# A fused transformer kernel on one Trainium2 core: the second and third group's layernorms in fixed order, their tiles in two product buffers, the third x group loaded ahead of Wk, and the first head sum two V chunks later

## The chip, the cores and the metric

The kernel runs on one core of one Trainium2 chip. The metric is the time on the device in microseconds (us) of one execution. Executions of one kernel mostly agree within 0.3%. The changes told of here are smaller than 1%, so that medians of several fast runs are compared, and the traces are read to a tenth of a microsecond.

## The reference

Two layers are applied twice to x of 2048 rows by 1024 columns (bf16). Layer A is a layernorm, a sliding-window attention with dilation and 32 heads, and a residual. Layer B is a layernorm, a feed-forward of width 3584 with GELU, and a residual.

```python
def _A_ref(x, wqkv, wo):                       # H = 32, Dh = 32, W = 8, dil = 2
    q, k, v = split_heads(x @ wqkv)            # (cut)
    idx = pos[:, None] - (jnp.arange(W) * dil)[None, :]   # 8 keys: s, s-2, ..., s-14
    logits = jnp.einsum("bhsd,bhswd->bhsw", q, kg) * scale
    attn = softmax(where(idx >= 0, logits, -1e9))
    o = jnp.einsum("bhsw,bhswd->bhsd", attn, vg)
    return merge_heads(o) @ wo
def _B_ref(x, w1, b1, w2, b2):
    return gelu(x @ w1 + b1) @ w2 + b2
x = x + _A_ref(_layernorm(x), A_wqkv, A_wo)
x = x + _B_ref(_layernorm(x), B_w1, B_b1, B_w2, B_b2)   # and both once more
```

## The kernel before

The 2048 rows are worked on in four groups of 512 (four tiles of 128 rows each); two layers make eight units, n = 0 to 7. What matters here is the first unit, some 70 us at the start, where everything has to be fetched and prepared at once.

TensorE (PE) makes Q, K and V of a group in 8 chunks each, by `gen_qkv`. One `yield` stands after each chunk, and `stage` runs "side" work after a numbered chunk. Chunks 0 to 7 are Q, 8 to 15 K, 16 to 23 V.

```python
def gen_qkv(n, parts=1, defer=False, qk_pool=None, v_late=False):
    ...
    wq = wq_first if n == 0 else load_qkv(0)
    wk = load_qkv(1)              # two loads of 1 MB
    if n == 0:
        ln_a(1)                   # layernorm of the second group
        load_x(2)                 # x of the third group
        wv = load_qkv(2)
    ...                           # 8 Q chunks
    for c in range(NCH):
        ps = qkv_chunk(wk, c, xnT)
        act.copy(kT[:, c, HALO:], ps[:])
        if not defer:
            new_prod(n, c)
        yield
    ...                           # 8 V chunks
```

The logits are not matmuls of Q and K. VectorE (DVE) multiplies Q with eight shifted views of K, chunk by chunk, into a product of 4096 columns, and adds the products pairwise in a tree. `head_sum` then has PE sum over the elements of a head with a matrix of zeros and ones. With `parts=2`, chunks 0 to 3 make a first sum and chunks 4 to 7 a second. Each product lives in one of the three buffers of the pool `bigp`.

```python
def new_prod(n, c):
    prod = bigp.tile([P, W, T], BF16, name="big")          # bufs=3
    vec.tensor_tensor(out=prod[:], in0=q_chunk_broadcast, in1=k_windows, op=ALU.mult)
    ...                            # adds to the tree after every second chunk
```

A layernorm is statistics on VectorE, rstd on GpSimd (POOL), the normalisation `xn` on VectorE, and a transposing DMA from `xn` to `xnT`, the form that PE reads. Here `xn` has three buffers of its own, and the tile framework's scheduler orders the instructions on VectorE:

```python
def ln_norm(t, mv, rstd):
    xn = lnp.tile([P, D], BF16, name="xn", bufs=3)
    vec.tensor_scalar(out=xn[:], in0=x[t][:], scalar1=mv[:, 0:1], scalar2=rstd[:],
                      op0=ALU.subtract, op1=ALU.mult)
    return xn
...
    sp.dma_start_transpose(xnT[:, tt, :, :], xn[:].rearrange("s (k p) -> s k p", p=P))
```

All loads and transposing DMAs (not the biases) are issued in order by one queue, SP's. The stages at the start:

```python
load_bias()                        # b1 and b2, on GpSimd's queue
with tc.tile_pool(name="early", bufs=1) as early:
    load_x(1)
    stage(gen_qkv(0, 2), sides=at(6, ln_a, 2, early) + at(7, load_x, 3)
          + at(14, transpose_bias) + at(19, head_sum, 0, False))   # first sum after V chunk 3
    q1 = gen_qkv(1, 2, defer=True, qk_pool=early)
    stage(q1, sides=at(5, attend, 0) + ...)                        # second sum in attend
```

Of the kernel before, what the change touches and what calls it, by code (L numbers as in the profile page):

```python
# [11 lines left out]
BF16 = mybir.dt.bfloat16  # L12
# [5 lines left out]
def kernel(  # L18
# [18 lines left out]
    P = 128  # L37
    _, S, D = A_x.shape
# [10 lines left out]
    NTT = T // P  # L49
# [20 lines left out]
    lnp = ctx.enter_context(tc.tile_pool(name="lnp", bufs=2))  # L70
    xnp = ctx.enter_context(tc.tile_pool(name="xnp", bufs=2))
    attp = ctx.enter_context(tc.tile_pool(name="attp", bufs=1))
    bigp = ctx.enter_context(tc.tile_pool(name="bigp", bufs=3))
# [30 lines left out]
    vec, act, pool, sp = InOrder(nc.vector), InOrder(nc.scalar), InOrder(nc.gpsimd), InOrder(nc.sync)  # L104
# [17 lines left out]
    def load_x(g, t0=0, t1=NTT):  # L122
        for tt in range(t0, t1):
            t = g * NTT + tt
            sp.dma_start(x[t][:], x_in[t * P:(t + 1) * P, :])

    def load_qkv(which):
        tiles = []
        for h in range(2):
            wt = wpool.tile([P, KD // 2, D], BF16, name="wt")  # L130
            sp.dma_start(wt[:], wqkv_v[:, h * (KD // 2):(h + 1) * (KD // 2), which * D:(which + 1) * D])
            tiles.append(wt)
        return tiles
# [41 lines left out]

    b1_rows = attp.tile([KF, P], BF16, name="abc")

    def load_bias():
        pool.dma_start(b1_rows[:], B_b1.rearrange("(j p) -> j p", p=P))
        pool.dma_start(b2bc[:], B_b2.unsqueeze(0).to_broadcast([P, D]))  # L180

    def transpose_bias():
# [5 lines left out]
    def ln_stats(t, mv=None, rstd=None, between=None):  # L188
        stats = lnp.tile([P, 2, 6], F32, name="stats")
        for h in range(2):  # L190
            vec.bn_stats(stats[:, h, :], x[t][:, h * HALF:(h + 1) * HALF])
            if h == 0 and between is not None:
                between()
        if mv is None:
            mv = lnp.tile([P, 2], F32, name="mv")
            rstd = lnp.tile([P, 1], F32, name="rstd")
        vec.bn_aggr(mv[:], stats[:])
        pool.tensor_tensor(out=rstd[:], in0=mv[:, 1:2], in1=eps_t[:], op=ALU.add)
        pool.tensor_tensor(out=rstd[:], in0=rstd[:], in1=mhalf[:], op=ALU.pow)
        return mv, rstd  # L200
# [2 lines left out]
        for tt in range(NTT):  # L203
            ln_stats(g * NTT + tt, mv_ahead[:, tt, :], rstd_ahead[:, tt, :])

    def ln_norm(t, mv, rstd):
        xn = lnp.tile([P, D], BF16, name="xn", bufs=3)
        vec.tensor_scalar(out=xn[:], in0=x[t][:], scalar1=mv[:, 0:1], scalar2=rstd[:], op0=ALU.subtract, op1=ALU.mult)
        return xn

    def transpose_on_pe(xn, out, pst=None, halves=1):
        if pst is None:
            pst = psum.tile([P, KD, P], BF16, name="acc", bufs=6)
        for k in range(KD):
            pe(nc.tensor.transpose(pst[:, k, :], xn[:, k * P:(k + 1) * P], ident[:]))  # L215
        n = KD // halves
        for h in range(halves):
            act.copy(out[:, h * n:(h + 1) * n, :], pst[:, h * n:(h + 1) * n, :])
# [7 lines left out]
    def ln_tile(t, tt, xnT, on_pe=False, ahead=False):  # L226
        mv, rstd = (mv_ahead[:, tt, :], rstd_ahead[:, tt, :]) if ahead else ln_stats(t)
        xn = ln_norm(t, mv, rstd)
        if on_pe:
            late.append((xn, xnT[:, tt, :, :]))  # L230
            return
        sp.dma_start_transpose(xnT[:, tt, :, :], xn[:].rearrange("s (k p) -> s k p", p=P))
# [28 lines left out]
    def new_xnT(pool=None):  # L261
        return (pool or xnp).tile([P, NTT, KD, P], BF16, name="xnT")
# [7 lines left out]
    xa = {}  # L270
    xb = {}

    def qkv_chunk(wts, c, xnT, ps=None, k0=0, k1=KD, t0=0, t1=NTT):
        if ps is None:
            ps = acc_tile()
        for k in range(k0, k1):
            mm(ps[:, t0 * P:t1 * P], lhsT=wts[k // (KD // 2)][:, k % (KD // 2), c::NCH], rhs=xnT[:, t0:t1, k, :],
               start=(k == 0 and t0 == 0), stop=(k == KD - 1), skip_group_check=t1 - t0 < NTT)
        return ps
# [21 lines left out]
    def new_prod(n, c):  # L301

        s = st[n]
        prod = bigp.tile([P, W, T], BF16, name="big")
        vec.tensor_tensor(out=prod[:], in0=s["qT"][:, c, :].unsqueeze(1).to_broadcast([P, W, T]), in1=win(s["kT"][:, c, :]), op=ALU.mult)
        tree = s["prods"]
        tree.append(prod)
        if c % 2 == 1:
            for _ in range(1 if c % (NCH // s["parts"]) == 1 else 2):
                b = tree.pop()  # L310
                vec.tensor_tensor(out=tree[-1][:], in0=tree[-1][:], in1=b[:], op=ALU.add)

    def gen_qkv(n, parts=1, defer=False, qk_pool=None, v_late=False):
        g = n % NG
        xnT = xa.pop(n)
        s = st[n]
        s["parts"] = parts
        s["prods"] = []
        qk_pool = qk_pool or attp
        wq = wq_first if n == 0 else load_qkv(0)  # L320
        wk = load_qkv(1)
        if n == 0:
            ln_a(1)
            load_x(2)
            wv = load_qkv(2)
        qT = qk_pool.tile([P, NCH, T], BF16, name="qT")
        first = {}
        for kq in range(4 if n == 0 else 0):
            for c in range(6):
                first[c] = qkv_chunk(wq, c, xnT, first.get(c), kq * (KD // 4), (kq + 1) * (KD // 4), 0, 2)  # L330
                if (kq, c) in ((1, 5), (2, 5)):
                    transpose_on_pe(*first_late.pop(0))
        for c in range(NCH):
            ps = qkv_chunk(wq, c, xnT, first[c], t0=2) if c in first else qkv_chunk(wq, c, xnT)
            act.copy(qT[:, c, :], ps[:])
            yield
        if n > 0 and not v_late:
            wv = load_qkv(2)
        kT = qk_pool.tile([P, NCH, HALO + T], BF16, name="kT")
        s["qT"], s["kT"] = qT, kT  # L340
        act.copy(kT[:, :, 0:HALO], (zhalo if g == 0 else khalo)[:])
# [6 lines that stand above are left out]
        if g + 1 < NG:  # L348
            act.copy(khalo[:], kT[:, :, T:T + HALO])
        vT = attp.tile([P, NCH, HALO + T], BF16, name="vT", bufs=2)  # L350
        s["vT"] = vT
        if v_late:
            wv = load_qkv(2)
        act.copy(vT[:, :, 0:HALO], (zhalo if g == 0 else vhalo)[:])
        for c in range(NCH):
            ps = qkv_chunk(wv, c, xnT)
            act.copy(vT[:, c, HALO:], ps[:])
            yield
        if g + 1 < NG:
            act.copy(vhalo[:], vT[:, :, T:T + HALO])  # L360
# [121 lines left out]
    def ln_a(n, pool=None, ahead=False):  # L482
        xa[n] = new_xnT(pool)
        for tt in range(NTT):
            ln_tile((n % NG) * NTT + tt, tt, xa[n], ahead=ahead)

    def stage(gen, count=None, sides=()):


        u = 0  # L490
        while count is None or u < count:
            if next(gen, gen) is gen:
                break
            for v, f in sides:
                if v == u:
                    f()
            u += 1
        for v, f in sides:
            if v >= u:
                f()  # L500

    def at(u, f, *args, **kwargs):
        return [(u, lambda: f(*args, **kwargs))]

    def each(f, n, u0, du, c0=0, c1=NCH):
        return [(int(u0 + du * (c - c0)), lambda c=c: f(n, c)) for c in range(c0, c1)]
# [4 lines left out]
    warm_up(16)  # L511
    ln_first()
    build_constants()
    load_bias()
    with tc.tile_pool(name="early", bufs=1) as early:
        load_x(1)
        stage(gen_qkv(0, 2), sides=at(6, ln_a, 2, early) + at(7, load_x, 3)
              + at(14, transpose_bias) + at(19, head_sum, 0, False))
        q1 = gen_qkv(1, 2, defer=True, qk_pool=early)
        stage(q1, sides=at(5, attend, 0) + at(5, spread, 0) + at(5, hold) + each(new_prod, 1, 8, 1, 0, 4) + each(av, 0, 12, 1))  # L520
        q2 = gen_qkv(2, defer=True)
        stage(q2, 18)
        stage(gen_wo(0, 2))
        stage(q2, sides=each(new_prod, 1, 0, 1, 4, 8) + at(3, head_sum, 1, False) + at(4, transpose_late))
# [11 lines left out]
    n = N - 2  # L536
# [35 lines left out]
```

## Time and profile before

| | before |
|---|---|
| time, median of 3 runs | 1248.69 us (1248.13 to 1249.0) |
| span of the profiled run | 1247.2 us |
| PE busy | 1235.8 us, 99% |
| PE's longest wait | 6.20 us, first head sum |

From the page of the kernel before, the busy table and the chain that ended last (engine, share of the span):

```profile
PE 1235.8 (99%) x5871; PEld 633.7 (51%) x5871; DVE 836.1 (67%) x864; ACT 306.2 (25%) x477; POOL 97.6 (8%) x215
...
PE 96%; DVE 1%; POOL 0%; issue 0%
```

PE is busy nearly always, so only its idle time, and time in which its clock is lowered, can be won. Who waited for whom, on PE (in total, number of times, longest, in us):

```profile
PE L L118 <- DVE big L93: 6.2, 1, 6.2
PE acc L118 <- DVE big L93: 1.1, 1, 1.1
```

One wait stands out. The timeline of PE shows where it lies (start, duration, what; the wait before it in brackets):

```profile
37.19 8.85 PE L118 MATMUL acc<-xnT,wt 128*128 128x512 bf16 x40
52.24 1.05 PE L118 MATMUL L<-big,smat 128*32 128x512 bf16 x8 [6.20 <-DVE big L93]
53.22 19.42 PE L118 MATMUL acc<-xnT,wt 128*128 128x512 bf16 x80
72.57 0.62 PE L118 MATMUL L<-big,smat 128*32 128x512 bf16 x8
```

PE is through with V chunk 3 at about 46.05 us, and can start the head sum (`L<-big,smat`) only at 52.24. The timeline of VectorE in the same stretch shows why its first sum is late:

```profile
23.30 0.55 DVE L93 TENSOR_SCALAR xn<-x,mv,rstd 128x1024 bf16<-128x1024 bf16 x1 [1.73 <-DMA xnT<-xn]
26.61 1.29 DVE L93 BATCH_NORM_STATS2 stats<-x 128x6 f32<-128x512 bf16 x2 [2.76 <-DMA x<-in_A_x_dram]
...
35.12 2.28 DVE L93 TENSOR_TENSOR big<-qT,kT 128x4096 bf16<-128x4096 bf16 x1
...
40.39 0.55 DVE L93 TENSOR_SCALAR xn<-x,mv,rstd 128x1024 bf16<-128x1024 bf16 x1 [0.71 <-POOL rstd L93]
...
47.57 4.62 DVE L93 TENSOR_TENSOR big<-big 128x4096 bf16<-128x4096 bf16 x2
```

Tiles of the layernorm wait for a transposing DMA to give back an `xn` buffer (1.73 us) and for x of the third group (2.76 us). The first product (`big<-qT,kT`) starts at 35.12, with a layernorm still between the products, and the last add ends at 52.19.

The wait has a second cost. In windows of 1 us each (the third number from the end is the granted clock of TensorE):

```profile
50.00:51.00 1.00, 0.00 (x0) 0.00 (x0) 1.00 (x1) 0.00 (x0) 0.00 (x0) 0.70 1.06 401
51.00:52.00 1.00, 0.00 (x0) 0.00 (x0) 1.00 (x1) 0.00 (x0) 0.00 (x0) 0.50 1.05 387
...
57.00:58.00 1.00, 1.00 (x5) 0.60 (x4) 1.00 (x1) 0.48 (x1) 0.00 (x0) 0.89 0.00 0
```

The clock falls to half after 4.3 us of idleness, and some of the work after the wait runs at half speed.

### The profile page before, as it was taken

How to read it: one execution, taken by the hardware profiler on the slowest of the kernel's cores; microseconds unless marked ns; L12 is line 12 of the kernel's file. 1: busy time of each engine (PE TensorE's matmuls, PEld its weight loads, DVE VectorE, ACT ScalarE, POOL GpSimd, SP SyncE). 2: the span in 40 equal slices, each digit the busy share in tenths (PEclk: the TensorE clock that was granted, in tenths of full speed). 3: DMA queues.
4: the chain of work that ended last, by engine and by line, in shares of the span. 5: the costliest groups of instructions: out<-in, count | busy, mean ns of one | idle time of the engine just before them, and what ended most of it. 6: DMA issues, size and time to landing. Idle time of an engine off the chain costs nothing.

```text
span 1247.2 us, 14104 instructions
## 1 busy us (share of the span) xinstructions
PE 1235.8 (99%) x5871; PEld 633.7 (51%) x5871; DVE 836.1 (67%) x864; ACT 306.2 (25%) x477; POOL 97.6 (8%) x215
## 2 busy tenths in 40 slices
PE   9899999999999999999999999999999999999998
PEld 6466544446444564445644456444554444444444
DVE  6979879996995889518994279933598688012001
ACT  3243253003430035201342013510234101310310
POOL 3110112002001100101001010000000002000000
PEclk9899999999999999999999999999999999999999
DMA  9755464586746547656566465666644567546441
GB/s 299 215 190 190 122 201 157 162 211 194 198 146 204 162 142 205 184 164 165 162 192 199 165 159 178 164 192 195 198 153 151 181 202 190 169 152 198 144 140 55
DMA packets 215328, 219.83 MB, mean 176 GB/s; under 512 B 66066, under 2 KB 184992, under 8 KB 212192
## 3 DMA queue, kind: packets, MB, share of 16 engines
q1 hardware_dynamic: 212592, 208.16, 55.6%
q0 software_dynamic: 2672, 10.76, 2.8%
q8 instruction: 46, 0.75, 0.2%
q14 instruction: 18, 0.15, 0.0%
HBM read 197.40 MB, written 6.29 MB: 163 GB/s over the span
## 4 chain that ended last, share of the span: by engine, by line
PE 96%; DVE 1%; POOL 0%; issue 0%
PE acc L118 95%; DVE big L93 1%; PE L L118 1%; POOL rstd L93 0%; DVE xn L93 0%; PE acc L215 0%; DVE stats L93 0%; DVE x L93 0%; DVE mv L93 0%
## 5 line engine op out<-in xcount | busy, mean ns | idle before, releaser
L118 PE MATMUL acc<-xnT,wt 128*128 128x512 bf16 (+1 forms) x3376 | 724.3, 377 | 0.7 <-ACT xnT L93 0.7
L118 PEld LDWEIGHTS <-wt 128*128 128x128 bf16 x3376 | 398.5, 119 | 323.0 <-issue 7.0
L118 PE MATMUL acc<-wt,hT 128*128 128x512 bf16 (+1 forms) x1820 | 388.1, 376 | 0.0
L118 PEld LDWEIGHTS <-hT 128*128 128x128 bf16 x1820 | 178.1, 98 | 208.9
L93 DVE TENSOR_TENSOR big<-big 128x2048 bf16<-128x2048 bf16 (+2 forms) x182 | 239.3, 1346 | 1.6
L93 ACT ACTIVATE hT<-acc,b1T 128x512 bf16<-128x512 f32 x224 | 151.7, 687 | 318.4 <-PE acc L118 318.1
L93 DVE TENSOR_TENSOR big<-abc,vT 128x4096 bf16<-128x4096 bf16 x64 | 143.8, 2280 | 48.1 <-DMA abc<-a_d 48.1
L93 DVE TENSOR_TENSOR big<-qT,kT 128x4096 bf16<-128x4096 bf16 x64 | 143.8, 2284 | 24.4 <-ACT kT L93 23.8
L93 DVE TENSOR_TENSOR tmp<-acc,b2bc 128x512 f32<-128x512 f32 x56 | 38.6, 690 | 178.9 <-PE acc L118 175.2
L93 ACT CAST qT<-acc 128x512 bf16<-128x512 f32 x64 | 37.3, 586 | 327.4 <-PE acc L118 327.4
L118 PE MATMUL acc<-wt,oT 128*128 128x512 bf16 x448 | 97.9, 379 | 0.0
L93 DVE BATCH_NORM_STATS2 stats<-x 128x6 f32<-128x512 bf16 x128 | 84.1, 677 | 6.1 <-DMA x<-in_A_x_dram 5.3
L118 PEld LDWEIGHTS <-oT 128*128 128x128 bf16 x448 | 43.8, 98 | 52.9 <-issue 0.2
L93 DVE TENSOR_TENSOR x<-acc,big 128x512 bf16<-128x512 f32 (+1 forms) x9 | 5.7, 632 | 90.0 <-PE acc L118 90.0
L93 ACT CAST vT<-acc 128x512 bf16<-128x512 f32 x64 | 37.5, 586 | 93.4 <-PE acc L118 93.4
L93 DVE TENSOR_SCALAR xn<-x,mv,rstd 128x1024 bf16<-128x1024 bf16 x60 | 32.7, 545 | 36.6 <-POOL rstd L93 33.9
L93 POOL TENSOR_TENSOR rstd<-mv,eps_t 128x1 f32<-128x1 f32 x60 | 17.1, 285 | 509.6 <-DVE mv L93 509.6
L93 ACT CAST kT<-acc 128x512 bf16<-128x512 f32 x64 | 37.5, 586 | 73.0 <-PE acc L118 73.0
L93 POOL DMA_DIRECT2D a_d<-a x32 | 19.6, 639 | 404.9 <-DVE a L93 404.9
L93 DVE TENSOR_TENSOR x<-acc,x 128x512 bf16<-128x512 f32 x64 | 43.0, 671 | 6.8 <-PE acc L118 6.5
L93 DVE TENSOR_TENSOR x<-tmp,x 128x512 bf16<-128x512 f32 x56 | 38.7, 690 | 1.7
L93 POOL TENSOR_TENSOR rstd<-rstd,mhalf 128x1 f32<-128x1 f32 x60 | 33.9, 566 | 4.7
(54 smaller groups left out, 213.7 us busy)
## 6 DMA issues: line engine op xcount, KB each, us to landing
wt<-in_B_w_dram SPq DMA_DIRECT2D x56, 1024.0 KB, 5.8
wt<-in_B_w_dram SPq DMA_DIRECT2D x64, 896.0 KB, 4.8
wt<-in_A_wqkv_dram SPq DMA_DIRECT2D x46, 1024.0 KB, 5.7
wt<-in_A_wo_dram SPq DMA_DIRECT2D x16, 1024.0 KB, 5.0
abc<-a_d POOLq DMA_DIRECT2D x32, 256.0 KB, 5.0
x<-in_A_x_dram SPq DMA_DIRECT2D x16, 256.0 KB, 3.5
out_dram<-x SPq DMA_DIRECT2D x31, 128.0 KB, 1.8
wt<-in_A_wqkv_dram SPq DMA_DIRECT2D x4, 512.0 KB, 7.3
```

The source lines that it names most:

```text
L93: inst = f(*args, **kwargs)
L118: return pe(nc.tensor.matmul(*args, **kwargs))
```

## The change

The intent is to have VectorE's first sum ready sooner and to ask for it later. The second and third group's layernorms run in the fixed order of the program. Their normalised tiles go to two of the three product buffers, idle at that time, so that none waits for a transposing DMA. The third group's x is loaded ahead of Wk, Wv ahead of the third group's layernorm. The first head sum moves from after V chunk 3 (u = 19) to after V chunk 5 (u = 21). Two smaller moves come with it: b1 is loaded earlier and b2 later.

```diff
--- before.py
+++ after.py
@@ -175,8 +175,9 @@
 
     b1_rows = attp.tile([KF, P], BF16, name="abc")
 
-    def load_bias():
-        pool.dma_start(b1_rows[:], B_b1.rearrange("(j p) -> j p", p=P))
+    pool.dma_start(b1_rows[:], B_b1.rearrange("(j p) -> j p", p=P))
+
+    def load_b2():
         pool.dma_start(b2bc[:], B_b2.unsqueeze(0).to_broadcast([P, D]))
 
     def transpose_bias():
@@ -203,8 +204,9 @@
         for tt in range(NTT):
             ln_stats(g * NTT + tt, mv_ahead[:, tt, :], rstd_ahead[:, tt, :])
 
-    def ln_norm(t, mv, rstd):
-        xn = lnp.tile([P, D], BF16, name="xn", bufs=3)
+    def ln_norm(t, mv, rstd, xn=None):
+        if xn is None:
+            xn = lnp.tile([P, D], BF16, name="xn", bufs=3)
         vec.tensor_scalar(out=xn[:], in0=x[t][:], scalar1=mv[:, 0:1], scalar2=rstd[:], op0=ALU.subtract, op1=ALU.mult)
         return xn
 
@@ -310,7 +312,7 @@
                 b = tree.pop()
                 vec.tensor_tensor(out=tree[-1][:], in0=tree[-1][:], in1=b[:], op=ALU.add)
 
-    def gen_qkv(n, parts=1, defer=False, qk_pool=None, v_late=False):
+    def gen_qkv(n, parts=1, defer=False, qk_pool=None, v_late=False, qk_next=None):
         g = n % NG
         xnT = xa.pop(n)
         s = st[n]
@@ -320,9 +322,10 @@
         wq = wq_first if n == 0 else load_qkv(0)
         wk = load_qkv(1)
         if n == 0:
-            ln_a(1)
-            load_x(2)
+            ln_early(1)
             wv = load_qkv(2)
+            ln_early(2, qk_next)
+            load_x(3)
         qT = qk_pool.tile([P, NCH, T], BF16, name="qT")
         first = {}
         for kq in range(4 if n == 0 else 0):
@@ -484,6 +487,19 @@
         for tt in range(NTT):
             ln_tile((n % NG) * NTT + tt, tt, xa[n], ahead=ahead)
 
+    def ln_early(n, pool=None):
+
+        xa[n] = new_xnT(pool)
+        xns = bigp.tile([P, NTT, D], BF16, name="big")
+        vec.on = True
+        s = [ln_stats(n * NTT)]
+        for tt in range(NTT):
+            if tt + 1 < NTT:
+                s.append(ln_stats(n * NTT + tt + 1))
+            ln_norm(n * NTT + tt, *s[tt], xns[:, tt, :])
+            sp.dma_start_transpose(xa[n][:, tt, :, :], xns[:, tt, :].rearrange("s (k p) -> s k p", p=P))
+        vec.on = False
+
     def stage(gen, count=None, sides=()):
 
 
@@ -511,11 +527,10 @@
     warm_up(16)
     ln_first()
     build_constants()
-    load_bias()
     with tc.tile_pool(name="early", bufs=1) as early:
         load_x(1)
-        stage(gen_qkv(0, 2), sides=at(6, ln_a, 2, early) + at(7, load_x, 3)
-              + at(14, transpose_bias) + at(19, head_sum, 0, False))
+        load_x(2)
+        stage(gen_qkv(0, 2, qk_next=early), sides=at(14, transpose_bias) + at(14, load_b2) + at(21, head_sum, 0, False))
         q1 = gen_qkv(1, 2, defer=True, qk_pool=early)
         stage(q1, sides=at(5, attend, 0) + at(5, spread, 0) + at(5, hold) + each(new_prod, 1, 8, 1, 0, 4) + each(av, 0, 12, 1))
         q2 = gen_qkv(2, defer=True)
```

## The prediction

This was written before the changed kernel was run.

> **What bounds the kernel.** TensorE: the busy table gives PE 1235.8 of 1247.2 us (99%); the chain that ended last is 96% PE. Only PE's idle time (11.4 us) and time at a lowered clock can be won. The list of waits puts 6.20 us in one place: the first head-sum matmul waits for VectorE's product tree ("L <- DVE big: 6.2, 1 time").
>
> **The wait, by the timeline.** PE reaches the head sum after V chunk 3 at 46.05 us; VectorE finishes the sum of products 0 to 3 at 52.19; PE goes on at 52.24. VectorE is late because the second and third groups' layernorms stretch from 13.4 to 40.9 us: a gap of 1.73 us at 21.6 (buffer held by a transposing DMA), 2.76 us at 23.9 (third group's x, queued behind transposes), 0.93 us for rstd; the last normalisation falls between products. The first product starts at 35.12, though its K chunk was evicted at 27.4.
>
> The wait costs more than itself: in 1 us windows the granted clock falls to 0.50 at about 50.4 us and returns at 57.1. The Trainium skill, "TensorE: Matmul & The Clock Gate", Part 1, says that an idle window of about 3.4 us halves the clock and about 3.4 us of work restore it; this trace agrees in kind (4.3 us idle, then 4.9 us of slow work). From 52.24 to 72.57 PE did 8 + 80 matmuls in 20.33 us; at the rates elsewhere (8 in 0.55, 8 in 1.7256 us) they take 17.81. Loss 2.5 us. At stake: 8.7 us.
>
> **What the change does.** Third x moves ahead of Wk in a queue moving about 390 GB/s: Wk lands 2.6 us later, near 22.5; its halves are wanted at 25.1 and 26.0. VectorE runs both layernorms in order from 13.4 without buffer or x waits: per tile 2 x 0.62 + 0.12 + 0.46 = 1.8 us, 8 tiles and two 0.6 us tails: ends near 29.3. Then products without interruption, 4 x 2.24 + 3 x 2.28 = 15.8 us: first sum ready near 45.2, second near 61. The third product takes a buffer that the last transposing DMA must have read, by my estimate at 35 to 36 us, wanted at 36.0: 0 to 1 us lost.
>
> The first head sum, two units on, is reached 2 x 1.73 later, at 49.5: 4 us of slack, no wait, no clock drop. The second is reached at 72.57 - 8.7 = 63.9, against 61 to 62: 2 us of slack. Everything after moves with it, in unchanged order.
>
> So the whole 8.7 us is on the critical path and kept: 1248.7 - 8.7 = **1240.0 us**, range 1239.0 to 1242.2. Chances: faster by over 2% 0.003, within 2% 0.994, slower 0.003.
>
> **What would show it.** Right: no PE wait for products in the list of waits; clock 1.00 from 44 to 60; first product at 29 to 30 us; head sums on PE near 49.5 and 63.9. Wrong: a PE wait on Wk near 25 us; a VectorE gap over 2 us before the third product; a new PE wait at the second head sum.
>
> **What would make it wrong.** Wk late by over 2.5 us; third group's transposes late behind Wv's 2 MB; a second-head-sum wait of 1 to 3 us; a later weight-load wait that the 8.7 us had hidden. Each gives back a part. No other PE gap is touched, so hardly more than 8.9 us.

## The result, and the profile after

| | before | after |
|---|---|---|
| median of 4 runs each | 1248.85 us (1248.13 to 1249.69) | 1244.5 us (1243.05 to 1245.1) |
| ratio | | 0.9963 (95%: 0.9946 to 0.998) |
| span of the profiled run | 1247.2 us | 1243.4 us |
| PE's wait for the first head sum | 6.20 us | 2.72 us |
| clock at half | 50.4 to 57.2 us | 53.4 to 56.8 us |

Ratios here are the mean time of one kernel's fast runs over that of the other's in the same rounds, so not quite the ratio of the medians. The gain is 4.35 us by the medians and 3.8 by the profiles. That is half of what was predicted, and outside of the stated range. From the page after, busy table and chain:

```profile
PE 1235.0 (99%) x5871; PEld 633.6 (51%) x5871; DVE 836.8 (67%) x864; ACT 305.9 (25%) x477; POOL 94.1 (8%) x215
...
PE 96%; DVE 2%; DMA 1%; SPq 1%; issue 0%; POOL 0%; DVEq 0%
```

The waits of PE after:

```profile
PE L L118 <- DVE big L93: 2.7, 1, 2.7
```

PE's timeline after, at the two head sums:

```profile
37.56 12.31 PE L118 MATMUL acc<-xnT,wt 128*128 128x512 bf16 x56
52.58 0.61 PE L118 MATMUL L<-big,smat 128*32 128x512 bf16 x8 [2.72 <-DVE big L93]
53.13 15.72 PE L118 MATMUL acc<-xnT,wt 128*128 128x512 bf16 x64
68.78 0.61 PE L118 MATMUL L<-big,smat 128*32 128x512 bf16 x8
```

PE comes to the head sum at about 49.86, as predicted (49.5), and still waits, for VectorE. VectorE's timeline:

```profile
29.78 0.55 DVE L93 TENSOR_SCALAR big<-x,mv,rstd 128x1024 bf16<-128x1024 bf16 x1 [0.71 <-POOL rstd L93]
30.25 4.49 DVE L93 TENSOR_TENSOR big<-qT,kT 128x4096 bf16<-128x4096 bf16 x2
34.77 2.29 DVE L93 TENSOR_TENSOR big<-big 128x4096 bf16<-128x4096 bf16 x1
43.38 4.50 DVE L93 TENSOR_TENSOR big<-qT,kT 128x4096 bf16<-128x4096 bf16 x2 [6.33 <-DMA xnT<-big]
47.91 4.62 DVE L93 TENSOR_TENSOR big<-big 128x4096 bf16<-128x4096 bf16 x2
...
63.89 4.62 DVE L93 TENSOR_TENSOR big<-big 128x4096 bf16<-128x4096 bf16 x2
```

The layernorms do end at 30.3 and two products follow at once. Then VectorE stands idle for 6.33 us, until a transposing DMA (`xnT<-big`) lands. The third product wants the buffer in which the third group's normalised tiles lie, and these have not all been read yet. So the first sum is ready at 52.53, which is 0.34 us later than in the kernel before. What SP's queue did meanwhile (start and duration of the issues):

```profile
17.20 10.78 SPq L93 DMA_TRANSPOSE xnT<-big  x4
28.03 1.15 SPq L93 DMA_DIRECT2D wt<-in_A_wqkv_dram  x2
29.28 11.64 SPq L93 DMA_TRANSPOSE xnT<-big  x4
40.98 2.00 SPq L93 DMA_DIRECT2D x<-in_A_x_dram  x4
```

The second group's four transposing DMAs took from 17.20 to 27.98 to be issued. Wv came only then, and the third group's four behind it, until 40.92. Single issues and landings, read from the trace's records, tell more:

| issued by SP's queue, after | issue starts | issue takes | lands |
|---|---|---|---|
| Wk, first and second MB | 13.83, 14.49 | 0.38, 0.38 | 22.77, 25.42 |
| second group's transposes 1 to 4 | 17.20, 22.08, 25.35, 26.70 | 4.77, 3.18, 1.26, 1.28 | 26.42, 27.28, 28.63, 29.82 |
| Wv, first and second MB | 28.03, 28.70 | 0.57, 0.49 | 33.41, 38.58 |
| third group's transposes 1 to 4 | 29.28, 33.30, 38.29, 39.64 | 3.93, 4.89, 1.26, 1.28 | 39.47, 40.30, 41.67, 42.86 |

The first transpose behind Wk is issued until 21.97 and Wk's first MB lands at 22.77; the second until 25.26 and Wk's second MB lands at 25.42. Behind Wv it is the same: 33.21 and 33.41, 38.19 and 38.58. Nothing else that these issues wait for explains it: the tiles of these four had been normalised by 17.2, 19.0, 25.4 and 27.2 us, and the queue's own waits for earlier landings were over. So, as I read it, with two loads of 1 MB ahead, the issue of a transposing DMA itself is held until they are nearly done, and it blocks everything behind it on the queue. The experiments' profiles bear this out. In the change and in e2 to e8, the issue of the second group's second transpose ended 0.14 to 0.16 us before the last load ahead of it landed. In e8 that load was not Wk's second MB (landed at 21.53) but the last of the third group's x, put behind it (issue until 24.07, load landed at 24.23). What holds the issue is not shown by any trace; that it ends with the loads ahead is.

The kernel before had shown it already. The second group's second transpose, behind Wk, took 3.34 us to be issued, and the third group's first three, behind Wv, took 2.39, 2.81 and 2.05 us (with a wait of 1 us for a tile between them):

```profile
29.65 8.33 SPq L93 DMA_TRANSPOSE xnT<-xn  x3
```

The Trainium skill's "DMA: Bandwidth & Descriptors", section "Queues, rings and completion order", says that on each DMA engine the descriptors are consumed in ring order, though it promises no order of completion. Here the landings kept the order: wherever the third group's transposes were issued behind Wv, they landed after it.

Last, the clock after:

```profile
53.00:54.00 1.00, 1.00 (x7) 0.53 (x4) 1.00 (x1) 0.00 (x0) 0.00 (x0) 0.69 1.00 367
54.00:55.00 1.00, 1.00 (x4) 0.35 (x3) 1.00 (x2) 0.00 (x0) 0.00 (x0) 0.50 0.17 61
...
57.00:58.00 1.00, 1.00 (x6) 0.67 (x5) 1.00 (x1) 0.24 (x1) 0.00 (x0) 1.00 0.00 0
```

The sum of what is missing explains the difference of the profiles. PE's wait is 2.72 us. The half clock costs 1.85: from 52.58 to 68.78 PE did 8 head-sum and 64 other matmuls in 16.20 us, and at full clock they take 0.55 + 8 x 1.7256 = 14.35. The early part ran 0.37 us later in this run (the matmuls after the last of PE's own transposes began at 15.25 instead of 14.88). 8.7 - 2.72 - 1.85 - 0.37 = 3.8 us, and 1247.2 - 1243.4 = 3.8.

This sum holds for the profiled run, which was the slowest of the four. The record gives each run's mean granted clock. A spell of 3.41 us at half clock, as in this profile, makes it 0.999, and one of 6.83 us, as in the kernel before, 0.997. The four runs of the changed kernel have 0.999, 0.999, 1.0 and 1.0 (1245.1, 1244.42, 1244.58 and 1243.05 us), so that two of them had no such spell. How long PE waited in those is not known, for they were not profiled.

### The profile page after: what moved, and what is told of

It is laid out like the page before. It is cut to its first block, busy times and chain, and to the rows that moved or that the text cites. A ratio compares the mean times of both kernels' runs of the same rounds, so it can differ in the third digit from the quotient of the medians.

```text
span 1243.4 us, 14103 instructions
## 1 busy us (share of the span) xinstructions
PE 1235.0 (99%) x5871; PEld 633.6 (51%) x5871; DVE 836.8 (67%) x864; ACT 305.9 (25%) x477; POOL 94.1 (8%) x215
## 4 chain that ended last, share of the span: by engine, by line
PE 96%; DVE 2%; DMA 1%; SPq 1%; issue 0%; POOL 0%; DVEq 0%
PE acc L118 95%; DVE big L93 1%; DVE stats L93 1%; DMA x<-in_A_x_dram 1%; SPq L93 1%; PE L L118 0%; DMA xnT<-big 0%; POOL rstd L93 0%; DVE mv L93 0%; PE acc L217 0%; DVE x L93 0%; DVEq L93 0%
## 5 line engine op out<-in xcount | busy, mean ns | idle before, releaser
L93 DVE TENSOR_SCALAR xn<-x,mv,rstd 128x1024 bf16<-128x1024 bf16 x52 | 28.7, 551 | 31.3 <-POOL rstd L93 30.3
```

Of the source, the lines that this page charges most:

```text
L93: inst = f(*args, **kwargs)
```

## The experiments

Two theories stood at first. Theory A: the layernorm part gained nothing, for the third product waited for the last transposing DMA, held up behind Wv; all of the 4.4 us comes from asking for the sum later. Theory B: the layernorm part gave some of it. The kernels e1 to e4 ran in one set of rounds, e5 to e8 in another, all with 5 timed runs. All gave correct results.

| | median us (range) | ratio to before | 95% |
|---|---|---|---|
| before, first and second set | 1248.3 (1247.28 to 1249.89), 1248.24 (1247.78 to 1248.95) | | |
| e1, head sum moved only | 1244.51 (1243.66 to 1246.4) | 0.9969 | 0.9956 to 0.9981 |
| e2, all but the head sum | 1248.48 (1246.69 to 1249.13) | 0.9997 | 0.9984 to 1.0009 |
| e3, own buffers | 1240.33 (1240.11 to 1240.6) | 0.9934 | 0.9921 to 0.9946 |
| e4, Wv last | 1243.29 (1242.72 to 1246.8) | 0.996 | 0.9947 to 0.9974 |
| e5, b2 late | 1243.04 (1242.4 to 1244.07) | 0.9959 | 0.9946 to 0.9971 |
| e6, Wv last and b2 late | 1242.36 (1242.11 to 1242.46) | 0.9951 | 0.9939 to 0.9964 |
| e7, own buffers, head sum at 19 | 1240.67 (1240.3 to 1240.71) | 0.9937 | 0.9923 to 0.995 |
| e8, own buffers, x behind Wk | 1240.55 (1240.44 to 1240.75) | 0.9937 | 0.9925 to 0.995 |

### e1_head_sum_only: one part of the change alone

```diff
 # the kernel before
-    at(19, head_sum, 0, False)
+    at(21, head_sum, 0, False)
```

> The kernel before, with only the first head sum moved two V chunks on. Theory A (the whole gain of the change comes from this move; the layernorm part gave nothing, because VectorE's third product waited 6.3 us for the third group's last transposing DMA): VectorE's first sum stays at about 52.2 us, PE waits 2.7 us for it, the clock may drop once for 2 to 4 us, the second sum at 68.0 is reached about when it is ready; time 1243.5 to 1245.5, the same as the changed kernel within 1 us. Rival B (the layernorm part gave part of the 4.4 us): 1246 to 1247.5, at least 1.5 us slower than the changed kernel.

Measured: 1244.51 us, the same as the changed kernel's 1244.5. PE's wait:

```profile
PE L L118 <- DVE big L93: 3.0, 1, 3.0
```

VectorE's first sum was ready at 52.57. In the profiled run the half clock lasted 6.83 us, longer than I had expected, and that run was the slowest of the five; by their granted clock (1.0), three of the other four had no such spell. The move of the head sum alone gives what the change gave, to within about 1 us (the intervals of the two ratios, 0.9969 and 0.9963, overlap): theory A holds, and B, which had this run at least 1.5 us slower than the change, does not.

### e2_head_sum_at_19: the change without that part

```diff
 # the changed kernel
-    at(21, head_sum, 0, False)
+    at(19, head_sum, 0, False)
```

> The changed kernel with the head sum back at its old place. Theory A: PE comes at about 46.4 us, VectorE's sum at about 52.5, so a wait of about 6.1 us with a clock drop as in the kernel before; time 1248.5 to 1249.7, no gain. Rival B: the layernorm part alone is worth 1.5 us or more: 1247 or less.

Measured: 1248.48 us, no gain over before (0.9997, 95%: 0.9984 to 1.0009). The layernorm part alone is worth nothing that can be told from noise as it stands; the interval leaves room for 2 us at most. In the profiled run, the fastest of the five (1246.69), the queue ran about a microsecond earlier, so that VectorE's gap was 5.10 us and PE's wait was less than I had expected:

```profile
PE L L118 <- DVE big L93: 4.8, 1, 4.8
```

### e3_own_buffers: taking away what the third product waits for

The third group's tiles go to the three `xn` buffers and one further small one, and the third product's buffer stays free. The order of SP's queue is unchanged; the transposing DMAs are as late as ever.

```diff
 # the changed kernel, in ln_early
+        own = n == 2
-        xns = bigp.tile([P, NTT, D], BF16, name="big")
+        xns = None if own else bigp.tile([P, NTT, D], BF16, name="big")
 ...
+            if own:
+                xn = lnp.tile([P, D], BF16, name="xn", bufs=3) if tt < 3 else pool.tile([P, D], BF16, name="xn4")
+                xn = xn[:]
+            else:
+                xn = xns[:, tt, :]
-            ln_norm(n * NTT + tt, *s[tt], xns[:, tt, :])
-            sp.dma_start_transpose(xa[n][:, tt, :, :], xns[:, tt, :].rearrange(...))
+            ln_norm(n * NTT + tt, *s[tt], xn)
+            sp.dma_start_transpose(xa[n][:, tt, :, :], xn.rearrange(...))
```

> The changed kernel, with the third group's normalised tiles in four small buffers of their own instead of the third product buffer, so that no product waits for its transposes (the order on every queue is the same). Theory A: products run without a gap from about 30.3 us, first sum near 46, second near 62; PE waits at neither head sum (49.9 and 64.2); the clock stays at 1.00; time 1240.0 to 1241.2, the 8.7 us that were predicted less some 0.4 us of later start. Rival C (VectorE's chain is late for another cause, or the gain is given back later): a gap or a wait elsewhere, time above 1243.

Measured: 1240.33 us, as expected, and faster than both kernels. The last transposing DMA landed at 41.72 us, hardly sooner than the 42.86 of the changed kernel, but no product waits for it. VectorE's timeline (no idle time in brackets up to the second sum's end at 61.97):

```profile
30.05 6.69 DVE L93 TENSOR_TENSOR big<-qT,kT 128x4096 bf16<-128x4096 bf16 x3
...
41.37 4.62 DVE L93 TENSOR_TENSOR big<-big 128x4096 bf16<-128x4096 bf16 x2
...
57.35 4.62 DVE L93 TENSOR_TENSOR big<-big 128x4096 bf16<-128x4096 bf16 x2
```

PE comes to both head sums without a wait; its clock is at full speed until the very end:

```profile
49.41 0.61 PE L118 MATMUL L<-big,smat 128*32 128x512 bf16 x8
...
63.92 0.61 PE L118 MATMUL L<-big,smat 128*32 128x512 bf16 x8
```

The span is 1238.5 us, 8.7 below the first profile of before. So the 8.7 us were there and are kept to the end; rival C falls.

### e4_wv_last: taking Wv out of the transposes' way

```diff
 # the changed kernel, in gen_qkv
-            wv = load_qkv(2)
             ln_early(2, qk_next)
+            wv = load_qkv(2)
```

> The changed kernel, with the load of Wv issued after the third group's four transposes instead of before them. Theory A (the transposes were late because they stood behind Wv's 2 MB in the queue, and their issue itself is held up by the backlog): the four are issued from about 28.0 us at some 1.3 us each and have landed by about 36, so the third product starts at 37.1 without a gap; Wv lands at 36.5 and 39.5, wanted by PE at 39.9 and 40.7; no PE wait at the head sums, time 1240.0 to 1241.5. Rival D (transposes are slow in themselves, or were late because of the normalisation): the last lands after 40 us, a gap of over 3 us stays, time above 1243. If Wv is late, a PE wait near 40 us gives back 1 to 2 us.

Measured: 1243.29 us, half right. Without Wv ahead of them, the third group's first three transposes were issued in 1.28 to 1.34 us each (3.93, 4.89 and 1.26 in the changed kernel) and landed at 31.45, 32.64 and 36.01. So Wv ahead of them had held the issues, as theory A has it. But D is refuted only in part: the third landed after 5.2 us, and the fourth, issued in 2.44 us, only at 38.39, so that, as D foretold, a gap of over 3 us (3.88) stayed before the third product (the profile puts it down to ScalarE, but the product waits for several semaphores at once, and it started 0.7 us after that landing, as it did 0.5 us after it in the changed kernel), and Wv was now late itself, at 41.28 and 44.76. A new wait took what was won, and it twice stopped PE. SP's queue, VectorE's gap and PE's wait:

```profile
17.66 16.98 SPq L93 DMA_TRANSPOSE xnT<-big  x8
34.70 1.12 SPq L93 DMA_DIRECT2D wt<-in_A_wqkv_dram  x2
...
39.08 2.29 DVE L93 TENSOR_TENSOR big<-qT,kT 128x4096 bf16<-128x4096 bf16 x1 [3.88 <-ACT b1T L93]
...
PE acc L118 <- DMA wt<-in_A_wqkv_dram: 3.7, 2, 2.4
```

```profile
41.33 1.08 PE L118 MATMUL acc<-xnT,wt 128*128 128x512 bf16 x4 [1.35 <-DMA wt<-in_A_wqkv_dram]
44.81 11.30 PE L118 MATMUL acc<-xnT,wt 128*128 128x512 bf16 x44 [2.40 <-DMA wt<-in_A_wqkv_dram]
56.04 0.61 PE L118 MATMUL L<-big,smat 128*32 128x512 bf16 x8
```

The head sum at 56.04 no longer waits. The load of b2 (issued at 30.16, landed at 35.02) ran beside the slow transposes. That made b2 the next suspect, for the change had moved it there.

### e5_b2_late: the load of b2 put off

```diff
 # the changed kernel
-    ... + at(14, transpose_bias) + at(14, load_b2) + at(21, head_sum, 0, False)
+    ... + at(14, transpose_bias) + at(21, head_sum, 0, False)
-        stage(q2, 18)
+        stage(q2, 18, sides=at(0, load_b2))
```

> The changed kernel, with the load of b2 (which the change moved from about 15 to about 30 us, among the transposes) put off to after the first attention's loads; nothing else moves on SP's queue or VectorE. Theory A2 (the transposing DMAs stand behind Wv, and the b2 load adds to it, since it takes 6.8 us beside them): the last one lands at 40.5 to 42 instead of 42.9, the gap before the third product is 3.5 to 5 us instead of 6.3, the PE wait 0.5 to 2 us; time 1241.5 to 1243.5. Theory A (Wv alone): nothing moves, 1243 to 1245.

Measured: 1243.04 us. The ratio, 0.9959, is not to be told from that of the change (0.9963). In the profile the last transpose landed at 40.44, the gap was 3.84 us and the first head sum waited 0.27 us. But most of that is not b2's: in this run Wv was already issued at 26.57 instead of 28.03. From the issue of Wv to the last landing it took 13.87 us, against 14.17 to 16.16 in the profiles of the change, e2, e3, e7 and e8. So b2 costs some tenths of a microsecond up to perhaps one; how much exactly stays open. What the run does show is the next limit. With the first wait all but gone, PE waits at the second head sum, since VectorE has not made up for its gap:

```profile
50.17 0.61 PE L118 MATMUL L<-big,smat 128*32 128x512 bf16 x8 [0.27 <-DVE big L93]
...
66.15 0.61 PE L118 MATMUL L<-big,smat 128*32 128x512 bf16 x8 [1.40 <-DVE big L93]
```

### e6_wv_last_b2_late: both

The edits of e4 and e5 together.

> The changed kernel with Wv behind the transposes and b2 put off as well. Theory A2: the seventh and eighth transposes, which landed at 36.0 and 38.4 with the b2 load beside them, land at about 34 and 35.5; the gap before the third product falls from 3.9 to under 1 us; Wv lands near 38 and 41 instead of 41.3 and 44.8, so that PE waits 0 to 1 us for it instead of 3.7; time 1240.3 to 1241.8. Theory A (b2 doesn't matter): as with Wv last alone, 1243 to 1244.

Measured: 1242.36 us, a little better than e4 and short of what was expected. The fourth transpose landed at 36.47 instead of 38.39, and the gap before the third product was 2.51 us, not under 1. Wv landed at 39.03 and 41.71, so that PE waited 1.47 us for its second half:

```profile
41.76 9.72 PE L118 MATMUL acc<-xnT,wt 128*128 128x512 bf16 x44 [1.47 <-DMA wt<-in_A_wqkv_dram]
51.40 0.61 PE L118 MATMUL L<-big,smat 128*32 128x512 bf16 x8
```

So neither of the two orders tried frees both: either the transposes or Wv are late. Other orders, or a split of Wv around the transposes, were not tried. Why the fourth transpose took 4.94 us to land with Wv issued after it, while the third took 3.37, is left open.

### e7_own_buffers_at_19: is the later head sum needed?

```diff
 # the kernel e3
-    at(21, head_sum, 0, False)
+    at(19, head_sum, 0, False)
```

> The kernel with the third group's tiles in own buffers, with the head sum back at its old place. If the uninterrupted products alone are enough, VectorE's first sum at 46.0 meets PE at about 46.0: a wait of 0 to 0.5 us, no clock drop, second head sum at 64 without a wait; time 1240.2 to 1241. If the two units of delay are needed as well: a wait of over 1.5 us, time above 1242.

Measured: 1240.67 us, and no wait at the head sum; PE came to it at 46.46, and VectorE's last add had ended at 46.2:

```profile
41.59 4.62 DVE L93 TENSOR_TENSOR big<-big 128x4096 bf16<-128x4096 bf16 x2
...
46.46 0.62 PE L118 MATMUL L<-big,smat 128*32 128x512 bf16 x8
...
64.42 0.61 PE L118 MATMUL L<-big,smat 128*32 128x512 bf16 x8
```

With products that run through, the layernorm part alone is worth nearly all of the gain, with hardly any slack left. In the change it was worth nothing that the runs can tell. What the fixed order and the buffers are each worth was not tried.

### e8_own_buffers_x_after_wk: is the third x group's place needed?

```diff
 # the kernel e3
-        load_x(2)
         stage(gen_qkv(0, 2, qk_next=early), ...
 # in gen_qkv
+            load_x(2)
             ln_early(1)
```

> The kernel with own buffers, with the third x group loaded behind Wk again: its x lands at about 23 to 25.5 instead of 16.5 to 18.6, so VectorE waits 1 to 3 us for it and the first product starts at 31 to 33 instead of 30.1; first sum at 47 to 49, PE at 49.4: no wait. Second sum at 63 to 65 against PE at 63.9: a wait of 0 to 1.5 us. Time 1240.2 to 1241.8: the order of the loads is worth at most some 1.5 us once the buffers don't hold up the products. If the load order is essential: above 1243.

Measured: 1240.55 us, as e3. The last of x landed at 24.23 us instead of about 18.5, but VectorE was busy with the second group until about 22 anyway, so that the first product started at 30.47 against 30.05. I had expected VectorE to wait 1 to 3 us for x; it waited 0.28 us. The place of this load is worth nothing here.

## Why the prediction was wrong

- **What bounds the kernel, and what is at stake: right.** 8.7 us of PE's time hung on the first head sum, 6.2 by waiting and 2.5 by the half clock. In e3 both were gone and the span was 8.7 us shorter; by the medians of its rounds 8.0 us (1248.3 - 1240.33).
- **Layernorms end near 29.3 us: right.** They ended at 30.3, of which about 0.4 us is a later start.
- **Wk lands near 22.5: wrong, without harm to PE.** It landed at 25.42. That it would be about 2.6 us later was right (3.0 later than the 22.41 of before, 0.4 of it the later start), but 22.5 was the old time and not the old time plus 2.6. PE wanted the second half at about 26.4, so that it lost nothing: luck, for the prediction had put Wk 2.9 us too early. The queue did not get off so lightly: as read above, the second group's second transpose was held until Wk was nearly there (issue until 25.26, against 22.04 before), and Wv stood behind it.
- **"0 to 1 us lost" before the third product: wrong, and this is the step that failed.** I had the last transposing DMA read its buffer by 35 to 36 us; it landed at 42.86, and VectorE lost 6.33 us. The prediction does not show how it came to 35 to 36, but none of its terms is the time for which an issue is held. The traces show that a transposing DMA with two 1 MB loads ahead of it takes 3.2 to 4.9 us to be issued, where one takes 1.3 without them, and holds all that stand behind it. So Wv was issued at 28.0, and the third group's transposes came after it. The text names "transposes late behind Wv's 2 MB" as what would make it wrong, but gives it 1 us where it cost six. The hold is not all of it: with Wv out of the way the last landing was at 38.39 (e4), and with b2 put off as well at 36.47 (e6), still over the estimate; that rest stays open.
- **No wait at the first head sum, no clock drop: wrong, as a consequence.** 2.72 us and 1.85 us.
- **No wait at the second head sum: held in the profile, by a hair.** VectorE's sum was ready at 68.51, PE came at 68.78. In e5, where the first wait was 0.27 us, the second was 1.40.
- **Everything after moves with it: right.** No PE wait after the second head sum is in any of the lists of waits.
- **What the parts are worth was not asked.** I priced the change as a whole. e1 and e2 show that as run its whole gain, to within about 1 us, is the two units of delay; e3 and e7 that the layernorm part can gain nearly all by itself, if no product buffer hangs on a transposing DMA.

## What to carry to other kernels

A buffer that is idle now is only free for borrowing if its last reader is done when the owner comes back; where that reader is a DMA, count the bytes ahead of it on its queue, and the time for which its issue is held, and not only its own duration. Price the parts of a change one by one: here a part that only asks later and a part that delivers earlier aimed at the same wait, and the second gained nothing that the runs can tell. A wait of PE of a few microseconds can cost 0.4 to 0.7 of its length again by the clock (2.5 on 6.2 us before, 1.85 on 2.72 after), and that part differs from run to run: in two of the changed kernel's four runs there was no half-clock spell.

## What the Trainium skill lacked or had wrong

- "DMA: Bandwidth & Descriptors" (sections "DMA Transpose (X-bar)" and "Rules for kernel authors") says nothing of an issue that is held, and "Perfetto Trace Analysis" (section "DMA Instruction — HWDGE (DVE, Sync)") gives no figure for the waits that it draws within an issue. Here a transposing DMA's issue took 1.24 to 1.35 us on an empty or short queue and 3.2 to 4.9 us with two loads of 1 MB ahead, ending, in the profile after, 0.2 to 0.8 us before the first or second of them landed. Others lie between, at 1.8 to 3.1 us, and not all of these are explained. The plain loads around them took 0.3 to 0.6 us as a rule, but single ones 1.76 us (after, issued at 4.16 us) and 2.71 us (e4, at 41.35 us).
- "TensorE: Matmul & The Clock Gate" (section "Why this matters for your kernels") advises against idle gaps over about 3 us. Here a gap of 2.72 us (the changed kernel) and one of 2.40 that came 1.1 us after another of 1.35 (e4) were followed by a half-clock spell, while single gaps of 1.40 (e5) and 1.47 (e6) did not. Part 1 of the page says that the window runs freely; that agrees with half-clock spells of 3.41 us (after, e2, e4) and 6.83 us (before, e1), one or two windows of its 3413 ns, and with runs of one kernel that differ: e1's five have a mean granted clock of 0.997, 0.999 and three times 1.0. In the profile after, the clock fell at 53.4 us, 0.8 us after PE had gone on.
